# A spectral block kernel: normalized rows in a tile of their own, the second sequence's forward stages due later, one copy on ScalarE

## The chip, the cores and the metric

The kernel runs on one core of a Trainium2 chip. The core has TensorE (PE in the profile; PEld is its weight load), VectorE (DVE), ScalarE (ACT), GpSimd (POOL) and SyncE (SP), which here only issues DMA transfers. The metric is device time in microseconds of one launch.

## The reference

Eight sequences of 3136 rows of 256 float32 values go through two blocks. The second works on the output of the first.

```python
X = np.fft.rfft(x, axis=1)                    # over the rows
Yr = Xr @ w_r - Xi @ w_i + b_r
Yi = Xr @ w_i + Xi @ w_r + b_i
Y  = soft_threshold(Yr, 0.01) + 1j * soft_threshold(Yi, 0.01)
y  = np.fft.irfft(Y, n=3136, axis=1)          # output of the first block
...
mixed = np.real(fft(fft(y, axis=1), axis=2))  # over rows and columns
u  = y + mixed
un = (u - mean(u)) / np.sqrt(var(u) + 1e-6)   # over the columns
out = u + np.maximum(un @ w_ch1, 0) @ w_ch2   # 256 -> 1024 -> 256
```

`soft_threshold` stands for the two lines that shrink a value towards zero by 0.01. The weights `w_ch1` and `w_ch2` come to the kernel as 64-bit floats, which it converts itself.

## The kernel before

A transform over 3136 rows is done as 64 times 49. Every sequence passes through these steps, each a Python generator:

- `p1` (lines 339 to 371), the first forward stage: chunks of the input are loaded by SP (`xf`), multiplied by a 64-point transform matrix (L358 in sequence 1, in plain float32; three products of split values in `mm3`, L150 to L152, elsewhere), copied out of PSUM (`ev`, L366, alternately by ScalarE and VectorE) and stored to DRAM (`ad`, L369). Sequence 1 has twelve chunks, each with two loads and two stores.
- `p2_f2` (390 to 449), the second forward stage F2: in four quarters, loads of `ad` (`af`, L403) and of a table, 49-point transforms (L419), then splitting into a high and a low part. In some places the imaginary half is first copied to a tile `im` by ScalarE (L445), which VectorE then adds (L446).
- `p2_w` (451 to 488): products with `w_r` and `w_i` and the soft threshold. The name in PSUM is `g_w`.
- `p2_mix` (490 to 580): the transform over the columns of the spectrum (L538 for sequence 0, L541 and L543 for the others) and sums of its even and odd parts; at the end of a quarter GpSimd makes two sums (L555, L556), two large copies put them in place (L558 on ScalarE for the even half, L559 on VectorE for the odd half), and SP stores the result (`md`, L565 to L579).
- `p2_yt` and `p2_g2` (584 to 643): transposes and the first inverse transform (L636 for sequence 0), stored as `bd` (L642).
- `p3_norm` (654 to 702): SP loads two blocks of `bd` (`bf`, L669) and of `md` (`mt`, L673 and L675); ScalarE and GpSimd split `bf` (`bh`, `bl`); TensorE does the last inverse transform; VectorE adds the mix (L683) and makes the statistics; the normalized rows are written over `mt` (L700).
- `p3_tr` (704 to 721): TensorE transposes the normalized rows (L718), ScalarE and VectorE split them (`uth`, `utl`).
- `p3_mlp1` and `p3_mlp2` (723 to 759): the two MLP products, with `hh` and `hl` between them (L737 on ScalarE, L738 on VectorE), and the output.

Sequence 0 has its own variants: `p1_first`, and single float32 products instead of split ones in `p2_yt`, `p2_g2` and `p2_mix`. While it passes through, the constants are loaded and `weights` (761 to 773) loads the MLP's weights in eight parts and converts each from 64-bit to a split of two 32-bit parts in `split_double` (158 to 189), mostly on VectorE, with temporary tiles of the tags `mt` and `ut`.

The order of work is a plan written out by hand. Every generator yields the time at which its next piece is due, in units of T = 10000, and a heap takes the earliest (lines 776 to 785). One sequence takes one T: the MLP of sequence b is due from b + 2 to b + 3. The due times are built from constants:

```python
SHAPE0, STEP0 = (1.0, 1.069, 0.988), 0.13
SHAPE, STEP1, STEP = (0.395, 0.569, 0.36), 0.2, 0.25
START1, LEAD = 1.77, 1.48
MLAG, NRM, TR = 0.874, -1.239, -0.993
```

`clock2` (373 to 377) turns them into a start and a step for each quarter of the `p2` stages: sequence 0 starts at 1.0 T with a step of 0.13 T, sequence 1 at `START1` with `STEP1`, later sequences at b + 0.52 T with 0.25 T. SHAPE gives the length of F2, the start of W and the length of W, in steps. `clock3` places normalization, transposes and the MLP of a sequence. `p1` of sequence 1 is due in twelve chunks from 1.4 T over 0.38 T. The framework then assigns instructions to the queues with a simulated timeline, so that instructions can stand a little before or behind their due order; each engine's queue is worked off in order, SP's too. Semaphores between the engines come from the accesses to tiles.

Tiles with one tag share that tag's buffers. Tag `mt` has two buffers of 512 float32 values per partition and is used by the weights' conversion, a constant or two, and `p3_norm`. Tag `im` has two buffers. PSUM tiles `g` have four.

Of the kernel before, what the change touches and what calls it, by code (L numbers as in the profile page):

```python
# [10 lines left out]
F32 = mybir.dt.float32  # L11
# [3 lines left out]
ALU = mybir.AluOpType  # L15
# [4 lines left out]
D = 256  # L20
# [6 lines left out]
S = 50  # L27
# [92 lines left out]
T = 10000  # L120

SHAPE0, STEP0 = (1.0, 1.069, 0.988), 0.13
SHAPE, STEP1, STEP = (0.395, 0.569, 0.36), 0.2, 0.25
START1, LEAD = 1.77, 1.48
MLAG, NRM, TR = 0.874, -1.239, -0.993


# [1 line left out]
def spectral_block(ctx: ExitStack, tc: tile.TileContext, x, w_ri, b_ri, w1, w2,  # L129
# [28 lines left out]
    def split_double(name, h, l, sl, src):  # L158

        def tmp(tag, bufs, dt=I32):
            return sb.tile([128, 512], dt, tag=tag, bufs=bufs, name=f"cv_{name}_{tag}")

        raw = sb.tile([128, 1024], I32, tag="uth", bufs=2, name="raw_" + name)
        behind(1, out=raw.rearrange("p (f e) -> p f e", f=src.shape[1]), in_=src)
        lo, hi = raw[:, 0::2], raw[:, 1::2]
        tf = tmp("mt", 2, F32)
        sc.activation(tf, hi.bitcast(F32), AF.Abs)
        va.tensor_scalar(tf, tf, HI_MIN, HI_MAX, op0=ALU.max, op1=ALU.min)  # L170
        t = tf.bitcast(I32)
        va.tensor_scalar(t, t, 3, 0x7FFFFFFF, op0=ALU.logical_shift_left, op1=ALU.bitwise_and)
        w = tmp("ut", UTB)
        va.tensor_scalar(w, hi, -0x80000000, 0x40000000, op0=ALU.bitwise_and, op1=ALU.bitwise_or)
        va.tensor_tensor(w, w, t, op=ALU.bitwise_xor)
        wf = w.bitcast(F32)
        e = tmp("ut", UTB)
        va.tensor_scalar(e, w, -0x800000, None, op0=ALU.bitwise_and)
        r = tmp("mt", 2)
        va.tensor_scalar(r, lo, 8, None, op0=ALU.logical_shift_right)  # L180
        rf = tmp("ut", UTB, F32)
        va.scalar_tensor_tensor(rf, r, 2.0 ** -44, e.bitcast(F32), op0=ALU.mult, op1=ALU.mult)

        def v(t):
            return t.rearrange("p (f e) -> p f e", f=h[sl].shape[1]) if len(h[sl].shape) == 3 else t
        sc.copy(h[sl], v(wf))
        d = tmp("ut", UTB, F32)
        gp.tensor_sub(v(d), v(wf), h[sl].bitcast(F32))
        gp.tensor_add(l[sl], v(d), v(rf))
# [15 lines left out]
    def load_consts():  # L205
        yield 0.97 * T
        behind("x", out=fwd_f, in_=c_fwd)
        w_v = w_ri.rearrange("a (k p) e -> a p k e", p=128)
        for name, tag in (("wr", "hh"), ("ws", "hh"), ("wd", "hl")):
            KF[name] = sb.tile([128, 2, D], F32, tag=tag, bufs=2, name=name + "f")  # L210
        behind("x", out=KF["wr"], in_=w_v[0])
        wi = sb.tile([128, 2, D], F32, tag="mt", bufs=2, name="wi")
        behind("x", out=wi, in_=w_v[1])

        for name, sign in (("ws", -1.0), ("wd", 1.0)):
            va.scalar_tensor_tensor(KF[name], wi, sign, KF["wr"], op0=ALU.mult, op1=ALU.subtract)
        for name in ("wr", "ws", "wd"):
            split(name, KF[name])
        yield 0.99 * T
        KF["cs"] = sb.tile([128, 2, 129], F32, tag="hl", bufs=2, name="csf")  # L220
        behind("x", out=KF["cs"], in_=c_cs)
        yield 1.55 * T
        split("fwd", fwd_f)

        cs = K["cs"] = cp.tile([128, 2, 2, 128], F32R, name="cs")
        t = KF["cs"]
        sc.copy(cs[:, :, 0], t[:, :, 0:128])
        lo_v(cs[:, :, 1], t[:, :, 0:128], cs[:, :, 0])
        sc.copy(cs[:, 0, 1, 0:1], t[:, 0, 128:129])
        inv = sb.tile([128, 128], F32, tag="mt", bufs=2, name="inv_f")  # L230
        nc.sync.dma_start(out=inv, in_=c_inv)
        split("inv", inv)

# [105 lines left out]
    def p1(b):  # L339
# [6 lines left out]
                ad = dr.tile([N2, 2, U, D], F32, tag="ad", bufs=4, name=f"ad{i}")  # L346
                a_dram[i] = lambda u, ad=ad: (ad, u)
        todo = chunks + [(NM - 1, 1)] * (b % 2 == 0)
        t0, width = (1.4, 0.38) if b == 1 else (b - 0.3, 0.75)
        for ci, (m, n) in enumerate(todo):  # L350
            yield T * (t0 + width * ci / len(todo))
            w = n * D
# [37 lines left out]
    def p2_f2(b):  # L390


        for q in range(4):
# [17 lines left out]
            for ui in range(4):  # L411
# [23 lines left out]
                if ui < (3 if b else 2):  # L435
                    xx = sb.tile([128, 2, 2, 2, S], F32, tag="xx", bufs=2, name="xx")
                    xv_ = xx.rearrange("p k s c j -> p k s (c j)")
                    sc.copy(xv_, gv)
                    put(sc.copy, [Xh], xv_)
                    put(lo_g, [Xl, Xh], xv_)  # L440
                    va.tensor_add(xs, xx[:, :, :, 0], xx[:, :, :, 1])
                else:
                    im = sb.tile([128, 2, 2, S], F32, tag="im", bufs=2, name="im")
                    put(sc.copy, [Xh], gv)
                    sc.copy(im, gv[:, :, :, S:])  # L445
                    va.tensor_add(xs, gv[:, :, :, :S], im)  # L446
                    put(lo_v, [Xl, Xh], gv)
# [42 lines left out]
    def p2_mix(b):  # L490
# [12 lines left out]
        for q in range(4):  # L503
# [52 lines left out]
            gp.tensor_sub(mq[:, 0, :, 1, 1:], even[:, :, 1:], odd[:, :, 1:])  # L556
            sc.copy(mq[:, 0, :, 0, 0:1], even[:, :, 0:1])
            sc.copy(even[:, :, 1:], mq[:, 0, :, 1, 1:])  # L558
            va.tensor_copy(odd[:, :, 1:], mq[:, 0, :, 0, 1:])  # L559
            sc.copy(odd[:, :, 0:1], mq[:, 0, :, 1, 0:1])  # L560
            mr = mq.rearrange("p a u h e -> p a (u h e)")
            mp, mm = (mq[:, i].rearrange("p u h e -> p u (h e)") for i in range(2))
# [91 lines left out]
    def p3_norm(b):  # L654

        for gi, (g0, z) in enumerate(groups[b % 2]):
            t0, T3 = clock3(b, g0)
            for i, n in parts_of[z]:
# [5 lines left out]

                src = [(b - 1, m), (b, m)] if joint else [(b, m), (b, NM + m)]
                bf = sb.tile([128, 512], F32, tag="bf", bufs=2, name="bf")
                mt = sb.tile([128, 2, D], F32, tag="mt", bufs=2, name="mt")
                for r, (bb, n2) in enumerate(src):
                    nc.sync.dma_start(out=bf[r * 64:r * 64 + 64, :w].rearrange("p (n d) -> p n d", d=D),  # L669
                                      in_=n2_rows(b_dram[bb], n2, n))  # L670
# [25 lines left out]
                gp.tensor_mul(vv[:, :n], vv[:, :n], rs[:, :n])  # L696
                gp.tensor_scalar(vv[:, :n], vv[:, :n], -0.5, 1.5, op0=ALU.mult, op1=ALU.add)
                gp.tensor_mul(rs[:, :n], rs[:, :n], vv[:, :n])  # L698
                for j in range(n):
                    va.tensor_scalar(mt[:, j], ut[:, j], ag[:, j, 0:1], rs[:, j], op0=ALU.subtract, op1=ALU.mult)  # L700
                normed[b, gi, i] = mt
                uts[b, gi, i] = ut

    def p3_tr(b):
        for gi, (g0, z) in enumerate(groups[b % 2]):
            t0, T3 = clock3(b, g0)
            for i, n in parts_of[z]:
                yield t0 + T3 * (TR + i / 4)
                if i == 0:
                    uth = sb.tile([128, 2, 512], F32R, tag="uth", bufs=2, name="uth")  # L710
                    utl = sb.tile([128, 2, 512], F32R, tag="utl", bufs=2, name="utl")
                    uthl[b, gi] = uth, utl
                mt = normed.pop((b, gi, i))
                g = gtile("g_ut")
                gv = g.rearrange("p (k t) -> p k t", k=2)
                for j in range(n):
                    for k in range(2):
                        te.transpose(gv[:, k, j * 128:(j + 1) * 128], mt[:, j, k * 128:(k + 1) * 128], ident)  # L718
                tw = slice(i * 128, i * 128 + n * 128)
                sc.copy(uth[:, :, tw], gv[:, :, :n * 128])  # L720
                lo_v(utl[:, :, tw], gv[:, :, :n * 128], uth[:, :, tw])
# [101 lines left out]
```

## Time and profile before

| | us |
|---|---|
| median of 3 runs | 1958.12 |
| lowest and highest run | 1956.15, 1961.05 |
| the profiled execution, its time | 1961.45 |
| the profiled execution, its span | 1959.7 |

| engine | busy us | share of the span |
|---|---|---|
| TensorE, matmuls | 1856.2 | 95% |
| TensorE, weight loads | 1709.1 | 87% |
| VectorE | 1322.5 | 67% |
| ScalarE | 853.2 | 44% |
| GpSimd | 704.8 | 36% |

The granted TensorE clock is 0.969 on the mean of the span. The profile shows one execution. A line of the timeline gives start and duration in us, the engine, the kernel's line, the operation, its output and inputs by the program's names, and in brackets how long the engine was idle before it and what ended that. SPq is SyncE's queue of DMA issues; the duration there is that of the issue, not of the transfer. Ends of matmuls are modelled, so a busy TensorE is not one at its peak.

### The profile page before, as it was taken

The numbers are of one execution on the slowest core, as the hardware profiler recorded it, in microseconds if no ns is written. First come the engines' busy times: TensorE is split into PE (matmuls) and PEld (weight loads), VectorE is DVE, ScalarE is ACT, GpSimd is POOL, SyncE is SP. The second block draws the span as 40 slices with busy tenths as digits, with TensorE's granted clock in tenths as the row PEclk, the third lists the DMA queues.
The fourth block names the chain that finished last, engine by engine and source line by source line (L and its number), as shares of the span: only waits on it lengthen the run. The fifth ranks groups of instructions, "written<-read, shape, count | busy, mean of one in ns | idle before, by whom it ended". The sixth has DMA issues, their size and how long they took to land.

```text
span 1959.7 us, 35047 instructions
## 1 busy us (share of the span) xinstructions
PE 1856.2 (95%) x12115; PEld 1709.1 (87%) x12115; DVE 1322.5 (67%) x2831; ACT 853.2 (44%) x1888; POOL 704.8 (36%) x1087
## 2 busy tenths in 40 slices
PE   4875799999999999999999999999999999999999
PEld 3764699989999999998999999998999998998999
DVE  2676677777776777766677777766777766675543
ACT  2443544444444454443444544434544434433322
POOL 0345544344433444343333443323543322322210
PEclk7886899999999999999999999999999999999999
DMA  7466654345443544434443444435433332223210
GB/s 215 122 177 192 154 139 131 101 119 148 115 122 109 152 129 121 117 98 138 136 134 104 136 137 114 127 99 141 136 106 98 107 98 89 83 70 109 68 41 25
DMA packets 163540, 233.05 MB, mean 119 GB/s; under 512 B 27484, under 2 KB 107428, under 8 KB 163364
## 3 DMA queue, kind: packets, MB, share of 16 engines
q1 hardware_dynamic: 163364, 230.82, 41.9%
q8 instruction: 97, 1.59, 0.3%
q14 instruction: 79, 0.65, 0.1%
HBM read 127.95 MB, written 102.76 MB: 118 GB/s over the span
## 4 chain that ended last, share of the span: by engine, by line
PE 80%; DVE 7%; DMA 6%; SPq 3%; issue 2%; ACT 1%; POOL 1%; DVEq 0%; POOLq 0%; ACTq 0%
PE o L150 8%; PE o L151 8%; PE o L152 8%; PE h L150 8%; PE h L151 8%; PE h L152 8%; PE g_f L419 4%; PE g_w L150 3%; PE g_w L152 3%; PE g_w L151 3%; PE g_g L150 2%; PE g_g L152 2%; PE g_g L151 2%; PE g_yt L609 2%; PE g_ut L718 2%
## 5 line engine op out<-in xcount | busy, mean ns | idle before, releaser
L151 PE MATMUL o<-w2h,hl 128*128 128x256 f32 x1568 | 431.4, 285 | 8.4 <-DVE hl L738 8.4
L738 DVE SCALAR_TENSOR_TENSOR hl<-h,hh 128x512 fp32r<-128x512 f32 (+1 forms) x416 | 272.3, 655 | 243.8 <-ACT hh L737 242.5
L737 ACT ACTIVATE hh<-h 128x512 fp32r<-128x512 f32 (+1 forms) x416 | 238.0, 573 | 443.0 <-PE h L152 382.7
L152 PE MATMUL o<-w2h,hh 128*128 128x256 f32 x1568 | 424.2, 280 | 0.0
L150 PE MATMUL o<-w2l,hh 128*128 128x256 f32 x1568 | 397.6, 286 | 2.5 <-DVE ut L757 2.3
L150 PE MATMUL h<-utl,w1h 128*128 128x512 f32 (+1 forms) x832 | 323.5, 389 | 8.1 <-DVE hl L738 8.1
L152 PE MATMUL h<-uth,w1h 128*128 128x512 f32 (+1 forms) x832 | 317.0, 381 | 0.0
L151 PE MATMUL h<-uth,w1l 128*128 128x512 f32 (+1 forms) x832 | 316.6, 381 | 0.0
L151 PEld LDWEIGHTS o<-w2h,hl 128*128 128x128 f32 x1568 | 297.3, 190 | 14.8 <-DVE hl L738 10.3
L152 PEld LDWEIGHTS o<-w2h,hh 128*128 128x128 f32 x1568 | 297.0, 189 | 3.2
L150 PEld LDWEIGHTS o<-w2l,hh 128*128 128x128 f32 x1568 | 286.3, 189 | 15.1 <-ACT Xsh L428 2.9
L147 POOL TENSOR_TENSOR bl<-bf,bh 128x512 fp32r<-128x512 f32 x104 | 130.0, 1251 | 298.3 <-ACT bh L678 296.1
L419 PE MATMUL g_f<-tff,af 98*128 98x100 f32 x1024 | 155.2, 284 | 25.8 <-DMA tff<-c_tf 13.0
L419 PEld LDWEIGHTS g_f<-tff,af 98*128 98x128 f32 x1024 | 148.5, 204 | 34.2 <-issue 23.4
L152 PEld LDWEIGHTS h<-uth,w1h 128*128 128x128 f32 x832 | 156.8, 189 | 23.8
L150 PEld LDWEIGHTS h<-utl,w1h 128*128 128x128 f32 x832 | 157.0, 189 | 22.8 <-DVE hl L738 9.0
L147 POOL TENSOR_TENSOR xl<-xf,xh 128x512 fp32r<-128x512 f32 (+1 forms) x75 | 97.1, 1295 | 203.2 <-ACT xh L362 201.3
L151 PEld LDWEIGHTS h<-uth,w1l 128*128 128x128 f32 x832 | 157.3, 189 | 13.4
L683 DVE TENSOR_TENSOR ut<-g_g,mt 128x512 f32<-128x512 f32 x104 | 68.3, 657 | 104.9 <-PE g_g L152 67.9
L147 POOL TENSOR_TENSOR Xl<-xx,Xh 128x400 fp32r<-128x400 f32 (+1 forms) x96 | 106.3, 1110 | 89.6 <-ACT Xh L428 69.3
L147 POOL TENSOR_TENSOR Xsl<-xs,Xsh 128x200 fp32r<-128x200 f32 x120 | 76.9, 642 | 161.4 <-ACT Xsh L428 144.2
L700 DVE TENSOR_SCALAR mt<-ut,ag,rs 128x256 f32<-128x256 f32 x196 | 90.8, 502 | 48.9 <-POOL rs L698 48.6
(155 smaller groups left out, 3811.3 us busy)
## 6 DMA issues: line engine op xcount, KB each, us to landing
bd<-bev SPq DMA_DIRECT2D x128, 196.0 KB
af<-ad SPq DMA_DIRECT2D x62, 392.0 KB
bf<-bd SPq DMA_DIRECT2D x184, 128.0 KB
out_dram<-ut SPq DMA_DIRECT2D x92, 256.0 KB
xf<-in_x SPq DMA_DIRECT2D x176, 128.0 KB
ad<-ev SPq DMA_DIRECT2D x168, 128.0 KB
md<-mq SPq DMA_DIRECT2D x112, 192.0 KB
mt<-md SPq DMA_DIRECT2D x416, 32.0 KB
```

What stands on the lines that cost most here:

```text
L147: gp.tensor_sub(out_, full, hi.bitcast(F32))
L150: te.matmul(o, lh, rl, start=start, stop=False)
L151: te.matmul(o, ll, rh, start=False, stop=False)
L152: return te.matmul(o, lh, rh, start=False, stop=stop)
L419: te.matmul(g[:, o:o + 100], afs[s][:, ui * D + k * 128:ui * D + k * 128 + 128], tfs[s][:, ui], start=True, stop=True)
L609: te.transpose(gt[:100, (v * 2 + o) * 128:(v * 2 + o + 1) * 128], y[:, o, place].rearrange("p c j -> p (c j)"), ident)
L683: va.tensor_add(ut[:, :n], g[:, :w].rearrange("p (n d) -> p n d", d=D), mt[:, :n])
L700: va.tensor_scalar(mt[:, j], ut[:, j], ag[:, j, 0:1], rs[:, j], op0=ALU.subtract, op1=ALU.mult)
L718: te.transpose(gv[:, k, j * 128:(j + 1) * 128], mt[:, j, k * 128:(k + 1) * 128], ident)
L737: sc.activation(hh[:, :w], h[:, :w], AF.Relu)
L738: va.scalar_tensor_tensor(hl[:, :w], h[:, :w], 0.0, hh[:, :w].bitcast(F32), op0=ALU.max, op1=ALU.subtract)
```

## The change

Four things are changed.

1. `p3_norm` writes the normalized rows to a new tile `nm` instead of over `mt`, and `p3_tr` transposes `nm`. The new tile shares the tag `mt`, which gets three buffers instead of two everywhere. So `mt` itself is written by DMAs alone, and is read once.
2. The due times of sequence 1's two forward stages: `p1` from 1.56 T over 0.34 T (it was 1.4 T over 0.38 T); `START1` is 1.92 (1.77) and `STEP1` 0.175 (0.2), which holds for all of sequence 1's `p2` stages.
3. The tag `im` has one buffer instead of two.
4. For sequence 0 the copy of the odd half of the mix (L559) is on ScalarE; for the others it stays on VectorE.

```diff
-SHAPE, STEP1, STEP = (0.395, 0.569, 0.36), 0.2, 0.25
-START1, LEAD = 1.77, 1.48
+SHAPE, STEP1, STEP = (0.395, 0.569, 0.36), 0.175, 0.25
+START1, LEAD = 1.92, 1.48
...
-        tf = tmp("mt", 2, F32)
+        tf = tmp("mt", 3, F32)
...
-        t0, width = (1.4, 0.38) if b == 1 else (b - 0.3, 0.75)
+        t0, width = (1.56, 0.34) if b == 1 else (b - 0.3, 0.75)
...
-                    im = sb.tile([128, 2, 2, S], F32, tag="im", bufs=2, name="im")
+                    im = sb.tile([128, 2, 2, S], F32, tag="im", bufs=1, name="im")
...
-            va.tensor_copy(odd[:, :, 1:], mq[:, 0, :, 0, 1:])
+            (va.tensor_copy if b else sc.copy)(odd[:, :, 1:], mq[:, 0, :, 0, 1:])
...
-                mt = sb.tile([128, 2, D], F32, tag="mt", bufs=2, name="mt")
+                mt = sb.tile([128, 2, D], F32, tag="mt", bufs=3, name="mt")
...
+                nm = sb.tile([128, 2, D], F32, tag="mt", bufs=3, name="nm")
                 for j in range(n):
-                    va.tensor_scalar(mt[:, j], ut[:, j], ag[:, j, 0:1], rs[:, j], op0=ALU.subtract, op1=ALU.mult)
-                normed[b, gi, i] = mt
+                    va.tensor_scalar(nm[:, j], ut[:, j], ag[:, j, 0:1], rs[:, j], op0=ALU.subtract, op1=ALU.mult)
+                normed[b, gi, i] = nm
...
-                        te.transpose(gv[:, k, j * 128:(j + 1) * 128], mt[:, j, k * 128:(k + 1) * 128], ident)
+                        te.transpose(gv[:, k, j * 128:(j + 1) * 128], nm[:, j, k * 128:(k + 1) * 128], ident)
```

The other lines with the tag `mt` change its number of buffers only.

More of the change, by code (lines that the diff above doesn't have):

```diff
@@ L178, in split_double @@
         va.tensor_scalar(e, w, -0x800000, None, op0=ALU.bitwise_and)
-        r = tmp("mt", 2)
+        r = tmp("mt", 3)
         va.tensor_scalar(r, lo, 8, None, op0=ALU.logical_shift_right)
@@ L211, in load_consts @@
         behind("x", out=KF["wr"], in_=w_v[0])
-        wi = sb.tile([128, 2, D], F32, tag="mt", bufs=2, name="wi")
+        wi = sb.tile([128, 2, D], F32, tag="mt", bufs=3, name="wi")
         behind("x", out=wi, in_=w_v[1])
@@ L229, in load_consts @@
         sc.copy(cs[:, 0, 1, 0:1], t[:, 0, 128:129])
-        inv = sb.tile([128, 128], F32, tag="mt", bufs=2, name="inv_f")
+        inv = sb.tile([128, 128], F32, tag="mt", bufs=3, name="inv_f")
         nc.sync.dma_start(out=inv, in_=c_inv)
@@ L712, in p3_tr @@
                     uthl[b, gi] = uth, utl
-                mt = normed.pop((b, gi, i))
+                nm = normed.pop((b, gi, i))
                 g = gtile("g_ut")
```

## The prediction

> **What bounds the kernel now.** I read the page's strip of slices first, then the stages by windows, then TensorE's order of work in the one stage with gaps, and last the queues that hold it there.
>
> ```profile
> span 1959.7 us, 35047 instructions
> ...
> PE   4875799999999999999999999999999999999999
> ...
> PEclk7886899999999999999999999999999999999999
> ```
>
> ```profile
> 86.00:135.00 49.00, 40.31 (x185) 32.22 (x184) 39.93 (x77) 25.81 (x66) 24.44 (x24) 0.86 0.64 184
> 135.00:182.00 47.00, 27.90 (x91) 19.12 (x92) 29.89 (x51) 17.24 (x36) 18.50 (x13) 0.68 0.70 212
> 182.00:224.00 42.00, 21.26 (x96) 18.66 (x96) 21.40 (x39) 15.18 (x33) 21.03 (x29) 0.67 0.61 156
> 224.00:440.00 216.00, 212.92 (x1432) 196.40 (x1432) 168.40 (x343) 106.41 (x237) 93.70 (x132) 1.00 0.45 124
> ```
>
> The columns after the stretch are busy time of PE, PEld, DVE, ACT and POOL, then the granted clock. From 224 us on TensorE is busy 212.92 of 216 us at full clock, and the strip stays at 9 to the end. What is done there costs its full TensorE time and can hardly gain. Before 224 us TensorE idles 9, 19 and 21 us of the three stretches, at a clock of 0.86 to 0.67. So the end moves by one balance: how much earlier the saturated part begins, less the TensorE work that is no longer done by then. The saturated part begins with the first MLP product of sequence 0.
>
> ```profile
> 167.74 1.42 PE L358 MATMUL g_f<-xf,fwd_f 128*128 128x512 f32 x2
> ...
> 173.45 0.39 PE L152 MATMUL g_f<-xh,fwdh 128*128 128x512 f32 x1
> 177.48 1.15 PE L419 MATMUL g_f<-tff,af 98*128 98x100 f32 x4 [3.63 <-DMA af<-ad]
> 178.42 1.91 PE L636 MATMUL g_g<-yf,tif 100*98 100x256 f32 x4
> 180.12 1.07 PE L538 MATMUL g_mix<-csf,ef 128*100 128x129 f32 x4
> ...
> 208.63 0.66 PE L718 MATMUL g_ut<-ident,mt 128*128 128x128 f32 x2 [12.01 <-DVE mt L700]
> ...
> 213.46 0.44 PE L150 MATMUL g_w<-Xl,wsh 128*128 128x400 f32 x1
> ...
> 215.64 0.35 PE L152 MATMUL g_w<-Xh,wdh 128*128 128x400 f32 x1
> 217.36 0.41 PE L718 MATMUL g_ut<-ident,mt 128*128 128x128 f32 x2 [1.37 <-issue]
> ...
> 220.52 0.38 PE L718 MATMUL g_ut<-ident,mt 128*128 128x128 f32 x2
> ...
> 223.85 0.47 PE L150 MATMUL h<-utl,w1h 128*128 128x512 f32 x1
> ```
>
> TensorE works in order. At 177.48 us it stands for the first matmul of sequence 1's F2, and behind it stand the last inverse product (L636) and the last mix (L538) of sequence 0, on which normalization waits. Then 12 us pass at the first transpose, and 15.2 us more until the MLP starts at 223.85.
>
> ```profile
> 185.99 5.81 DVE L559 COPY mq<-mq 100x508 f32<-100x508 f32 x1 [1.16 <-POOL mq L556]
> ...
> 202.51 0.69 DVE L683 TENSOR_TENSOR ut<-g_g,mt 128x512 f32<-128x512 f32 x1 [10.71 <-DMA mt<-md]
> ```
>
> ```profile
> 188.15 0.61 ACT L558 COPY mq<-mq 100x508 f32<-100x508 f32 x1
> ```
>
> ```profile
> 189.02 2.50 POOL L147 TENSOR_TENSOR bl<-bf,bh 128x512 fp32r<-128x512 f32 x2
> ```
>
> ```profile
> 185.90 0.47 SPq L262 DMA_DIRECT2D tif<-c_ti  x1
> 191.87 0.32 SPq L565 DMA_DIRECT2D md<-mq  x1
> ...
> 198.32 0.33 SPq L673 DMA_DIRECT2D mt<-md  x1
> ```
>
> This is the chain in those 12 us: the copy at L559, the mix's store at 191.87, the load of it at 198.32, the addition at 202.51.
>
> **The copy on ScalarE.**
>
> ```profile
> L559 DVE COPY mq<-mq x32: 408/417/5811, 98.7 to 1765.3; 100x508 f32<-100x508 f32 x32
> ```
>
> The columns are lowest, median and highest duration in ns. The median is 0.42 us, the one on the chain 5.81. It ends at 191.80, right behind GpSimd's last of a run of operations (189.02 + 2.50 = 191.52). On ScalarE the like copy of the other half (L558) took 0.61 us in the same place, so the odd copy should too. ScalarE was late itself: L558 ended at 188.76. Behind it the odd copy ends at 189.4, which gains 2.4 us; begun at 185.99, as VectorE's was, it would gain 191.80 - 185.99 - 0.61 = 5.2. I take 3.0, nearer to the lower, since ScalarE's order holds casts that wait for loads. It adds a wait for GpSimd there, with the short copy of L560 and casts queued behind. The other three copies cost 0.2 us more each and stand beside other work.
>
> The Trainium skill (SBUF — State Buffer, "Who interferes with whom") says that VectorE and GpSimd share a port pair under an exclusive lock held for a whole instruction, and that ScalarE never waits. By that rule as worded the copy would lose one GpSimd instruction (2.50 / 2 = 1.25 us) and then run (0.42); moving it would gain about 1.1 us, and the sum below would be -5.0 instead of -6.9. The trace disagrees, since the copy was locked out to the end of the run, so this gets no chance of its own.
>
> **The first forward stage of sequence 1 (12 chunks of p1) moves** from 1.40..1.748 T to 1.56..1.872 T (T is the plan's unit, one sequence). Each chunk issues two loads and two stores on SP.
>
> ```profile
> L262 SPq DMA_DIRECT2D xf<-in_x x30: 466/521/1517, 89.3 to 177.6; - x30
> ```
>
> ```profile
> L369 SPq DMA_DIRECT2D ad<-ev x28: 574/622/1098, 91.3 to 175.9; - x28
> ```
>
> That is 2 x 0.52 + 2 x 0.62 = 2.3 us of SP a chunk, and 24 records of 0.75 us for 12 chunks, 1.5 us of TensorE each, with 11.2 us of idle time before them in all:
>
> ```profile
> L358 PE MATMUL g_f<-xf,fwd_f 128*128 128x512 f32 x24 | 15.9, 749 | 11.2 <-DMA ad<-ev 4.8 <-issue 3.2 <-ACT w2h L186 2.1
> ```
>
> Before 1.56 T six chunks leave (6 x 2.3 = 13.7 us of SP). Between there and the last mix of sequence 0 (1.784 T) there are eight instead of six, and four come behind it. What the six leave behind them matters through the weights:
>
> ```profile
> 141.66 1.67 SPq L262 DMA_DIRECT2D raw_w<-in_w  x2
> ```
>
> ```profile
> 145.71 1.25 DVE L174 TENSOR_SCALAR cv_w_ut<-raw_w 128x512 int32<-128x512 int32 x1 [0.16 <-DMA raw_w<-in_w]
> ...
> 168.12 0.69 DVE L182 SCALAR_TENSOR_TENSOR cv_w_ut<-cv_w_mt,cv_w_ut 128x512 f32<-128x512 int32 x1
> ```
>
> The second weight's raw data, due from 1.45 T, is loaded only at 141.66 us, behind chunks on SP, and its conversion fills VectorE from 145.71 to 168.8; ScalarE's casts wait for it, and TensorE's work behind them. With six chunks fewer in front, these loads come earlier into a stretch where VectorE idles 9 us of 49. The gain lies between 0 (the first stretch is not held by SP) and 13.7 (all of it is). Two more chunks later take 2 x 2.3 = 4.6 of that back at most. I take -5.0 net, near a third of the 13.7.
>
> **The second forward stage (F2, W and what follows)** starts at 1.92 T instead of 1.77, with a step of 0.175 T for 0.2. Sequence 0's last products are due at 1.777 and 1.784 T, so F2 now stands behind them. TensorE then reaches L636 at 173.45 + 0.39 = 173.84 instead of 178.42: -4.6 (0 if ScalarE's or a load's wait takes its place). W of the first quarter was due from 1.849 T and is due from 1.989. So it leaves the 15.2 us between first transpose and MLP: the second pair of transposes came at 220.52, 3.2 us behind the first pair at 217.36, with W's products between, and VectorE's W operations stood in the same queue. I take -3.5 (0 to -5).
>
> What the earlier start gives up: 36 products of W and a few of F2 move into the saturated part. Twelve run from 213.46 to 215.64 at 0.19 us apart, so 36 x 0.19 = 6.8 us, with eight F2 matmuls (about 0.9 us) +7.7. The chunks of p1 and the first quarter of F2 (due 1.92 to 1.98 T) still come before 2.0 T and move nothing.
>
> **The handover to normalization of sequence 1.**
>
> ```profile
> 426.81 0.69 DVE L683 TENSOR_TENSOR ut<-g_g,mt 128x512 f32<-128x512 f32 x1 [1.51 <-DMA mt<-md]
> ```
>
> The last mix of sequence 1 was due at 1.77 + 0.6 + 0.2 x 1.927 = 2.755 T and is at 1.92 + 0.525 + 0.175 x 1.927 = 2.782 T; normalization stays at 2.802. From 223.85 us (2.0 T) to 426.81 (2.802 T) a T is 253 us, so 6.8 us of slack go. VectorE already waited 1.5 us there. While it waits at L683, the hl subtractions (L738) queue behind it, and TensorE waits for hl. Cost 0 to +6.8; I take +1.0, since the MLP's product is due 0.2 T later.
>
> **The tiles.** A normalized row block now takes the third buffer of the tag. If buffers go round, the load two blocks on still waits for the same transposes, and a block's own load comes no earlier.
>
> ```profile
> PE g_ut L718 <- DVE mt L700: 13.2, 4, 12.0
> ```
>
> TensorE lost 13.2 us at the transposes, 12.0 of it at the first, where no buffer was short; so 0 to -1.2, taken as 0. With one `im` buffer, ScalarE's second `im` copy of a quarter of sequence 0 waits for VectorE's L446, with a cast (L428) queued behind:
>
> ```profile
> L446 DVE TENSOR_TENSOR xs<-g_f,im 128x200 f32<-128x200 f32 x9 | 3.3, 362 | 2.9 <-POOL Xsl L147 1.4 <-PE g_w L150 0.8 <-POOL Xl L147 0.7
> ```
>
> Four such waits of at most 0.36 us are 0 to +1.4; I take +0.5. Later sequences use `im` once a quarter, where the earlier use is long past.
>
> **The sum.** -3.0 - 5.0 - 4.6 - 3.5 = -16.1 for the earlier start; +7.7 + 1.0 + 0.5 = +9.2 against it; together -6.9. The profiled execution took 1961.45 us (span 1959.7), which gives 1954.6. It is 3.3 us above the median of the runs, 1958.12, so for the median I say 1951.2. What a measurement can tell from no change is 0.3%, 5.9 us.
>
> **Rivals.** *Slower: SP becomes the bound of the new place.* The six chunks' 13.7 us of SP time stand later, eight chunks in the tail of sequence 0's mix and four between its stores and normalization's loads, and SP works in order: a chunk's store waits for its copy, and the mt loads behind it. For it: in 182 to 224 us VectorE's 10.71 us wait at L683 ends with such a load. Against it: SP stood still for the 5.5 us between 186.37 and 191.87, and issues of four chunks replace those of F2. Its price: the -5.0 goes (the sum is then -1.9) and up to 13.7 comes, +11.8, or 1970. It decides from 7.8 us of the 13.7 on. Chance 0.19.
>
> *No change: the transfers set the start anyway.* The way from store to addition (191.87 to 202.51) stays, and what comes ahead is absorbed in it: -5.0 and -3.5 go, leaving -7.6 + 9.2 = +1.6, or 1959.7. For it: the chain there is DMA and waits, not work. Against it: the store's own time is set by the copy and the mix ahead of it. Chance 0.25.
>
> *Larger gain: the weights' conversion leaves the chain.* -13.7 instead of -5.0 gives -15.6, or 1942.5. For it: TensorE idles 19 of 47 us in just that stretch. Chance 0.12.
>
> **How the numbers follow.** The forecast, 1951.2, has 0.44; its own range is 1946 to 1956 from the bounds of the copy and of W's place. About 0.38 of it lies beyond 5.9 us, which with the larger gain makes 0.50 faster. Slower is the SP rival, 0.19; the rest, 0.31, lies within. The range goes from 1941, just past the larger gain, to 1964, which takes in no change and the nearer half of the slower case.
>
> **What would show it.** Right: the last L538 ahead of sequence 1's first L419; the odd copy on ScalarE at about 0.6 us and the first store of the last mix at once behind; the second weight's conversion begun before 140 us; the first MLP product some 12 to 19 us before 223.85, with W's first products behind it; from there to 440 us TensorE as full as now. Wrong: the first MLP product at 220 or later, SP's loads of mt behind stores of chunks, or a gap of several us on TensorE at the handover near 420.

## The result and the profile after

| | median us | lowest, highest | runs |
|---|---|---|---|
| before | 1957.13 | 1954.13, 1961.05 | 4 |
| after | 1984.43 | 1976.19, 1991.09 | 4 |

After to before the ratio is 1.0136, 95% interval 1.0092 to 1.018. The kernel became 27 us slower (18 to 35 by the interval), where 7 us faster was forecast (1951.2) and 1964 was the end of the range. The profiled execution of the changed kernel took 1986.48 us, with a span of 1984.7 and the same mean clock as before, 0.969. In the changed kernel the lines behind 698 have a number higher by one.

The windows of the changed kernel, in the same stretches (columns as in the prediction):

```profile
86.00:135.00 49.00, 32.33 (x161) 26.66 (x160) 38.51 (x69) 23.74 (x63) 25.56 (x24) 0.83 0.43 133
135.00:182.00 47.00, 29.11 (x105) 19.18 (x103) 31.27 (x55) 19.99 (x44) 19.06 (x13) 0.75 0.70 197
182.00:224.00 42.00, 15.15 (x35) 8.86 (x36) 9.07 (x21) 9.55 (x17) 12.17 (x19) 0.58 0.65 178
224.00:440.00 216.00, 211.21 (x1399) 195.97 (x1398) 161.08 (x335) 104.74 (x236) 89.98 (x128) 0.99 0.43 119
```

The third row is the loss at the start: 35 TensorE records instead of 96, and VectorE busy for 9.07 us instead of 21.40. Some 40 of these records are products of sequence 1's F2 and W that the change means to move behind the start of the MLP; the rest is time lost. The chunks that left the first stretch show there as a DMA share of 0.43 instead of 0.64, and as nothing else that got faster. TensorE's order of work in the place of the loss:

```profile
178.96 0.61 PE L538 MATMUL g_mix<-csf,ef 128*100 128x129 f32 x4
...
199.45 0.69 PE L719 MATMUL g_ut<-ident,nm 128*128 128x128 f32 x2 [4.14 <-DVE nm L701]
...
208.96 0.79 PE L150 MATMUL g_f<-xl,fwdh 128*128 128x512 f32 x1 [5.45 <-POOL xl L147]
...
210.40 0.63 PE L150 MATMUL g_g<-bl,invh 128*128 128x512 f32 x1
...
220.84 0.66 PE L719 MATMUL g_ut<-ident,nm 128*128 128x128 f32 x2 [8.96 <-DVE nm L701]
...
229.60 0.39 PE L150 MATMUL h<-utl,w1h 128*128 128x512 f32 x1
```

The first transpose comes 9.2 us earlier than before (199.45 for 208.63), and the MLP starts 5.75 us later (229.60 for 223.85). So 15.2 us between the two have become 30.15. Only this distance can be relied on: single traces put the whole start a few us earlier or later. Two traces of one and the same kernel below (mt3_only, mt3_1280) start the MLP at 222.12 and 229.03 us, and pad_only, which changes no due time, has its first transpose at 198.12. The distance is 12.6 to 16.3 us in all twelve traces with the due times of before, and 30.1 in a second trace with the changed ones (after_1280). The second block's product starts at 210.40, no earlier than before (210.37), although the first block is earlier, and its transposes at 220.84 come later than the 217.36 of before. ScalarE's queue shows by what:

```profile
184.08 0.61 ACT L559 COPY mq<-mq 100x508 f32<-100x508 f32 x1
...
206.95 0.62 ACT L362 CAST xh<-xf 128x512 fp32r<-128x512 f32 x1 [3.14 <-DMA xf<-in_x]
...
215.20 0.62 ACT L362 CAST xh<-xf 128x512 fp32r<-128x512 f32 x1 [7.64 <-DMA xf<-in_x]
215.73 0.29 ACT L691 ACTIVATE rs<-ag,eps_t 128x2 f32<-128x2 f32 x1
```

The casts of L362 belong to chunks of sequence 2 (those of sequence 1 are not cast). Each waits for a load, and the first keeps TensorE from the second block's product until 208.96 + 1.44 = 210.40, the second keeps its `rs` until 215.73. In the issues of that stretch, 182 to 224 us, before and after, chunk loads have become 15 instead of 4:

```profile
xf<-in_x SPq DMA_DIRECT2D x4, 128.0 KB
```

```profile
xf<-in_x SPq DMA_DIRECT2D x15, 128.0 KB
```

The second half of the loss shows in no gap. The 128x256 products of the second MLP matmul, before and after (columns: busy us, mean ns, idle before):

```profile
L152 PE MATMUL o<-w2h,hh 128*128 128x256 f32 x1568 | 424.2, 280 | 0.0
```

```profile
L152 PE MATMUL o<-w2h,hh 128*128 128x256 f32 x1568 | 429.6, 283 | 0.0
```

There are three such forms, 4704 matmuls. From the starts of some 4000 pairs of neighbours that follow without a gap, the next one comes 115.8 ns after the last before the change and 118.4 ns after the change; 4704 times 2.6 ns is 12.2 us. Which matmuls these are, and why they are slower, the experiments had to show.

### The profile page after: what moved, and what is told of

Same layout as the page of the kernel before. It is cut to its first block, busy times and chain, and to the rows that moved or that the text cites. A ratio compares the mean times of both kernels' runs of the same rounds, so it can differ in the third digit from the quotient of the medians.

```text
span 1984.7 us, 34704 instructions
## 1 busy us (share of the span) xinstructions
PE 1866.7 (94%) x12115; PEld 1715.7 (86%) x12115; DVE 1308.9 (66%) x2827; ACT 854.4 (43%) x1892; POOL 702.9 (35%) x1087
## 4 chain that ended last, share of the span: by engine, by line
PE 79%; DVE 5%; DMA 4%; SPq 2%; ACT 1%; issue 1%; POOL 1%; DVEq 0%; POOLq 0%; ACTq 0%
PE o L151 9%; PE o L150 8%; PE o L152 8%; PE h L150 8%; PE h L152 8%; PE h L151 8%; PE g_f L419 4%; PE g_w L150 3%; PE g_w L152 3%; PE g_w L151 3%; PE g_g L150 2%; PE g_yt L609 2%; PE g_g L152 2%; PE g_g L151 2%; PE g_ut L719 2%; PE g_mix L541 1%
## 5 line engine op out<-in xcount | busy, mean ns | idle before, releaser
L151 PE MATMUL o<-w2h,hl 128*128 128x256 f32 x1568 | 436.8, 287 | 7.3 <-DVE hl L739 6.9
L152 PE MATMUL o<-w2h,hh 128*128 128x256 f32 x1568 | 429.6, 283 | 0.0
L701 DVE TENSOR_SCALAR nm<-ut,ag,rs 128x256 f32<-128x256 f32 x196 | 88.7, 491 | 60.8 <-POOL rs L698 60.3
```

The lines of the kernel that those rows point to most:

```text
L151: te.matmul(o, ll, rh, start=False, stop=False)
L152: return te.matmul(o, lh, rh, start=False, stop=stop)
L701: va.tensor_scalar(nm[:, j], ut[:, j], ag[:, j, 0:1], rs[:, j], op0=ALU.subtract, op1=ALU.mult)
```

## The experiments

Each version was timed beside the kernel before on the same chip. Single executions of one kernel lie 10 us and more apart (before: 1949.6 to 1963.5 over all series), so the medians decide, and a trace is used for where things stand.

| version | median us | before us | ratio, 95% interval |
|---|---|---|---|
| copy_only | 1955.92 | 1958.43 | 0.9991, 0.9974 to 1.0008 |
| tile_only | 1980.20 | 1958.43 | 1.0108, 1.0088 to 1.0127 |
| late_only | 1977.48 | 1958.43 | 1.0094, 1.0077 to 1.0111 |
| tile_copy | 1976.99 | 1958.43 | 1.0092, 1.0075 to 1.0108 |
| pad_only | 1968.56 | 1956.97 | 1.0053, 1.0032 to 1.0074 |
| mt3_only | 1976.22 | 1956.97 | 1.0096, 1.0078 to 1.0115 |
| late_f2 | 1964.26 | 1956.97 | 1.0030, 1.0015 to 1.0045 |
| late_p1 | 1978.37 | 1956.97 | 1.0106, 1.0083 to 1.0130 |
| pad_32 | 1967.65 | 1956.72 | 1.0060, 1.0042 to 1.0077 |
| tile_1280 | 1970.70 | 1956.72 | 1.0074, 1.0052 to 1.0096 |
| im_only | 1956.65 | 1956.72 | 1.0001, 0.9989 to 1.0013 |
| copy_all | 1947.79 | 1956.72 | 0.9955, 0.9938 to 0.9971 |
| after_1280 | 1975.47 | 1957.55 | 1.0092, 1.0071 to 1.0113 |
| mt3_1280 (= mt3_only) | 1976.88 | 1957.55 | 1.0094, 1.0073 to 1.0114 |
| late_p1_p2 | 1967.14 | 1957.55 | 1.0053, 1.0037 to 1.0070 |
| copy_all_p2 | 1940.68 | 1957.55 | 0.9914, 0.9896 to 0.9933 |
| mt3_pad32 | 1965.39 | 1957.80 | 1.0041, 1.0023 to 1.0060 |
| best_pad64 | 1954.03 | 1958.19 | 0.9986, 0.9973 to 0.9999 |

Differences in us below are a ratio's excess times 1957.

### Which part costs it

Three theories: the later due times cost it (D), the new tile costs it (T), or any edit shifts the queues and costs something (R).

**The copy alone.**

```diff
-            va.tensor_copy(odd[:, :, 1:], mq[:, 0, :, 0, 1:])
+            (va.tensor_copy if b else sc.copy)(odd[:, :, 1:], mq[:, 0, :, 0, 1:])
```

> The kernel before with one change: the odd copy of sequence 0 on ScalarE. Theory D (the later due times cost the time): faster by 3 to 7 us against before, since in the changed kernel the store of the last mix left at 184.75 us and not at 191.87. Theory T (the new tile costs it): the same 3 to 7 us faster. Theory R (any edit reorders the queues, and the order found is a matter of luck): anything from 8 us faster to 15 us slower.

Measured -1.8 us (-5.1 to +1.6): no loss, and a gain that can't be told from none.

**The tile alone**: `nm`, three buffers of `mt`, one of `im`.

> The kernel before with the tile nm, three buffers of tag mt and one of im; due times and copy as before. Theory D: within 6 us of before. Theory T: slower by 12 us or more, with the loads of mt later at the first blocks. Theory R: anything within 15 us.

**The due times alone**: `p1` of sequence 1, `START1` and `STEP1`.

> The kernel before with the later due times of sequence 1's two forward stages alone (p1 at 1.56 T, START1 1.92, STEP1 0.175). Theory D: slower by 25 to 35 us against before, the first MLP product at 230 to 240 us and 90 to 110 matmuls fewer done by 250 us. Theory T: slower by less than 12 us. Theory R: slower by 0 to 20 us.

**All but the due times.**

> The changed kernel with the due times of before (tile and copy stay). Theory D: faster than before by 2 to 8 us, so 30 us faster than the changed kernel. Theory T: slower than before by 5 us or more. Theory R: not the sum of the copy alone and the tile alone.

The tile costs +21 (17 to 25), the due times +18 (15 to 22), all but the due times +18 (15 to 21). So neither D nor T is the cause alone: two halves, each about as large. D also missed the size of its own half (+18, not 25 to 35, with the first MLP product at 224.02). R fell: tile and copy together cost what they cost alone (+18 for 21 - 2), and the tile alone lies beyond R's 15 us. Together they would be more than the changed kernel's +27, whose interval ends at 35; that the two losses overlap is likely, but was not shown.

### The tile's half: the place in memory

The tile changes no due time, and TensorE was slower by a steady 2.5 ns a matmul, so the first suspect was where the tiles lie. Three buffers of `mt` (+2048 bytes per partition) and one of `im` (-800) move the tiles of most tags that are first used later by 1248 bytes, the second weight's `w2h` and `w2l` among them; `hh` and `hl` stay.

**A tile that nobody uses, and nothing else.**

```diff
+        pad = sb.tile([128, 312], F32, tag="pad", bufs=1, name="pad")
+        gp.memset(pad, 0.0)
         wi = sb.tile([128, 2, D], F32, tag="mt", bufs=2, name="wi")
```

> The kernel before with one unused tile of 1248 bytes per partition ahead of the tag mt. From mt on, all tiles of later tags stand 1248 bytes higher, as they do with the three buffers of mt and the one of im; nothing else is changed. In the runs with the tile the 128x256 matmuls of the second MLP product start 2.4 ns later behind one another than before in quiet stretches, 4704 x 2.4 ns = 11 us of the +21. Theory P (the place of the tiles in memory slows these matmuls): +8 to +12 us here, and their mean goes from 280 to 283 ns. Theory Q (the order in the queues, which the new tile changes, makes all of it): 0, within 3 us of before, mean 280 ns. Theory B (the number of buffers itself): 0 as well.

Measured +10 us (6 to 14). Theory P held: 118.3 ns from start to start, as with the tile. Of the matmuls outside `o`, the pairs most frequent in the trace (`h`, `g_f`, `g_yt`, `g_ut`) kept their distance within 0.2 ns; of these, `h` and `g_yt` have operands that don't move, so only the other two say anything.

**Three buffers of `mt` and one of `im`, without `nm`.**

> The tag mt with three buffers and im with one, but the normalized rows still written over mt. TensorE's queue is that of before but for some 20 places, and the tiles stand at the addresses of the changed kernel. Theory P (place in memory): +8 to +12 us, the 128x256 matmuls at 283 ns. Theory B (a third buffer lets loads run ahead and collide, or the single im costs): +15 us or more, as with the new tile. Theory Q (only the new tile, since only it changes the order in the queues): within 3 us of before.

Measured +19 (15 to 23): nearly the tile's whole loss, with the rows still written over `mt`. So more than the place is lost without `nm`.

**A pad of 32 bytes.** The diff is that of the first pad, with 8 values instead of 312.

> The kernel before with one unused tile of 32 bytes per partition ahead of the tag mt. The second weight's tiles w2h and w2l begin at 193,440 and 201,632 bytes in the kernel before, 32 bytes past a multiple of 64; with the pad of 1248 bytes they began at a multiple of 64, every row of them alike cost the 128x256 matmuls 2.5 ns more, and the median rose by 10 us. Theory A (the address within 64 bytes decides): here they begin at a multiple of 64 too: +8 to +12 us, and o<-w2h,hh at 282 ns. Theory D (the distance decides, by which region of the memory the tiles come to lie in): a shift of 32 bytes does nothing, within 3 us of before and 280 ns.

+12 (8 to 15), theory A. A shift of 32 bytes does what the shift of 1248 did; it is not which region of the memory the tiles lie in. The rows of `w2h` are 1024 bytes apart, so each has the same address within 128 bytes.

**The tile with a pad of 32 bytes**, which moves the rest by 1280 bytes instead of 1248.

```diff
+        pad = sb.tile([128, 8], F32, tag="pad", bufs=1, name="pad")
+        gp.memset(pad, 0.0)
         wi = sb.tile([128, 2, D], F32, tag="mt", bufs=3, name="wi")
```

> The new tile with three buffers of mt and one of im, due times and copy as before, and an unused tile of 32 bytes ahead of mt: the tiles behind it are moved by 1280 bytes instead of 1248, so w2h and w2l lie 32 bytes past a multiple of 64 as in the kernel before. Theory A (address within 64 bytes): the 128x256 matmuls are back at 280 ns, and of the tile's +21 us about 11 go: +8 to +12. Theory D (distance): +18 to +22 as with the tile alone.

+14 (10 to 19), 7 less than the tile alone; theory A expected up to +12. The matmuls are back at 280 ns:

```profile
L152 PE MATMUL o<-w2h,hh 128*128 128x256 f32 x1568 | 424.3, 280 | 0.0
```

**The same in the changed kernel.**

> The changed kernel with an unused tile of 32 bytes ahead of mt, so that w2h and w2l lie 32 bytes past a multiple of 64 again. Theory A (the address within 64 bytes costs 4704 matmuls 2.5 ns each): 10 to 13 us less than the changed kernel, that is +13 to +18 over before, and o<-w2h,hh at 280 ns instead of 283. If the place matters only together with the other due times: +22 to +28.

+18 (14 to 22) where the changed kernel had +27 (18 to 35). The intervals overlap, but the row shows the effect itself: 280 ns, where the changed kernel had 283.

```profile
L152 PE MATMUL o<-w2h,hh 128*128 128x256 f32 x1568 | 425.2, 280 | 0.0
```

**A pad of 64 bytes** on the fastest version (below).

> The fastest version so far (the copy of the odd half on ScalarE for all sequences, sequence 2's chunks from 2.0 T over 0.45 T; -16.9 us) with an unused tile of 64 bytes ahead of mt: w2h and w2l begin 96 bytes past a multiple of 128, which is again 32 past a multiple of 64. Theory A64 (64 bytes decide): o<-w2h,hh at 279 to 280 ns and 1938 to 1944 us. Theory A128 (only 32 past a multiple of 128 is fast): 282 ns and 1949 to 1955 us.

Theory A64 fell, A128 held: +13 us against the 1940.68 of another series, and

```profile
L152 PE MATMUL o<-w2h,hh 128*128 128x256 f32 x1568 | 430.0, 283 | 0.0
```

with 119.0 ns from start to start. Together, by where `w2h` begins past a multiple of 128 bytes: at 0 (pad_only, the tile, the changed kernel) 118.3 to 118.4 ns; at 32 (before, tile_1280, after_1280, mt3_pad32) 115.7 to 115.9; at 64 (pad_32) 118.2; at 96 (best_pad64) 119.0. `hh` and `hl`, the other operand, began at 96 in all runs. Whether the address itself decides or its distance from the other operand's was not tried.

### The tile's half: the rest

**One buffer of `im` alone**, with a pad of 800 bytes so that nothing behind `im` moves.

```diff
-                    im = sb.tile([128, 2, 2, S], F32, tag="im", bufs=2, name="im")
+                    im = sb.tile([128, 2, 2, S], F32, tag="im", bufs=1, name="im")
```

> The kernel before with one buffer of im, and an unused tile of 800 bytes so that all tiles behind it stay where they are. With three buffers of mt and one of im the time rose by 19 us, of which the place in memory explains 10. Theory I (the single im makes the other 9: ScalarE's second copy of a quarter waits for VectorE's addition, with the casts for W behind it): +6 to +10 us. Theory M (the third buffer makes it: loads run ahead and change what stands in the queues): within 3 us of before.

+0.2 us (-2 to +3): the single `im` costs nothing.

**Three buffers of `mt` without the change of place.** The run under the label mt3_1280 was given the kernel without the small pad, so it only repeats mt3_only (+18, 14 to 22); the kernel meant is mt3_pad32.

> Three buffers of mt, one of im, rows still written over mt, and the unused tile of 32 bytes. Without that tile it was +19, of which 11 are the place. Theory M (a third buffer alone costs the other 8, by another order of loads): +6 to +10. Theory Q (the rest needs the new tile): within 3 us of before. The single im alone has been measured at nothing.

> Three buffers of mt, one of im, rows still written over mt, and the unused tile of 32 bytes, so that w2h and w2l lie 32 bytes past a multiple of 64 as before. Without the small tile this kernel was +19 in two series. Theory M (the third buffer by itself costs what the place doesn't explain): +6 to +10. Theory Q (the rest needs the new tile): within 3 us of before.

+8 (4 to 12): theory M. The third buffer costs something by itself. What the new tile adds to that, tile_1280 less mt3_pad32, is about 6, and the intervals overlap. What the tile changes is seen in SP's waits (us in total, times, longest). Before, with mt3_pad32, and with tile_1280 (whose line numbers are higher by two):

```profile
SPq L673 <- PE g_ut L718: 137.6, 54, 6.0
SPq L669 <- POOL bl L147: 81.9, 27, 9.6
```

```profile
SPq L675 <- PE g_ut L720: 106.0, 41, 6.0
SPq L671 <- POOL bl L147: 75.8, 23, 9.6
```

```profile
SPq L671 <- POOL bl L147: 138.0, 35, 9.6
...
SPq L675 <- PE g_ut L721: 3.9, 3, 3.2
```

SP hardly waits for transposes any more before it loads `mt`. The dependency is still there: in the built program the tag's three buffers go round, and a load of `mt` waits for the transposes of the rows two blocks back. But in SP's queue a load of `mt` now mostly stands behind the `bf` loads of three further blocks, where it stood behind those of two. SP waits there for a `bf` buffer, and by then the transposes are mostly done. TensorE gains nothing by that, and at the handover near 430 us the queues' new order is seen to hurt. ScalarE and TensorE with tile_only:

```profile
430.67 0.62 ACT L678 CAST bh<-bf 128x512 fp32r<-128x512 f32 x1 [4.20 <-DMA bf<-bd]
...
431.62 0.59 ACT L738 ACTIVATE hh<-h 128x512 fp32r<-128x512 f32 x1
```

```profile
432.26 0.50 PE L150 MATMUL o<-w2l,hh 128*128 128x256 f32 x2 [3.27 <-ACT hh L738]
```

A normalization cast stands for a load of `bf` ahead of `hh`, and TensorE waits 3.27 us (4.17 in tile_copy, 3.60 in tile_1280). Before, the gap there was 0.77 us, and 1.85 to 1.87 in copy_only, im_only, pad_only and pad_32. So it is 1 to 3 us at that one place; how the 14 us are made up was not settled.

### The due times' half

**The second stage alone** (`START1`, `STEP1`).

> The kernel before with START1 1.92 and STEP1 0.175 alone; the first forward stage of sequence 1 stays at 1.4 T. Theory S (the moved chunks cost it: their loads are slow, and their casts stand in ScalarE's queue ahead of the second block's normalization): the first MLP product comes before 218 us and the time is -3 to +4 us. Theory G (the work given up costs it: F2 and W of sequence 1 leave the gaps, and the MLP does not start earlier for it): first MLP product at 222 to 226 us, +8 to +15 us. Theory H (the later second stage meets the normalization of sequence 1): a gap of 4 us or more on TensorE between 400 and 450 us.

+6 us (3 to 9), between theory S (up to +4) and theory G (from +8). TensorE's order in late_f2:

```profile
194.62 0.66 PE L718 MATMUL g_ut<-ident,mt 128*128 128x128 f32 x2 [8.32 <-DVE mt L700]
...
203.24 0.66 PE L718 MATMUL g_ut<-ident,mt 128*128 128x128 f32 x2 [5.18 <-issue]
203.69 1.87 PE L419 MATMUL g_f<-tff,af 98*128 98x100 f32 x8
...
211.76 1.86 PE L419 MATMUL g_f<-tff,af 98*128 98x100 f32 x8
...
214.74 0.42 PE L150 MATMUL h<-utl,w1h 128*128 128x512 f32 x1
```

W's products have left the place between the first transpose and the MLP, but the 32 matmul records of sequence 1's first F2 quarter stand there in their stead, as they do in the changed kernel (221.30 to 229.04). The distance is 20.1 us, where it was 15.2, and 41 matmul records fewer are done when the MLP begins (581 for 622; 36 of W and 8 of F2 fewer, 3 others more). The MLP itself starts at 214.74; that is 9.1 us earlier than in the trace of before, but inside the 213.56 to 229.03 of the nine traces with the copy and the due times of before, so it isn't shown that the start is earlier at all. Windows of before, of im_only (whose time and due times are those of before) and of late_f2:

```profile
0.00:250.00 250.00, 171.35 (x801) 139.95 (x802) 144.59 (x280) 104.33 (x248) 93.23 (x118) 0.79 0.61 172
...
350.00:450.00 100.00, 97.64 (x650) 89.46 (x650) 74.09 (x151) 46.18 (x103) 41.55 (x58) 1.00 0.44 124
```

```profile
0.00:250.00 250.00, 169.77 (x822) 138.64 (x823) 145.43 (x285) 104.74 (x250) 91.76 (x119) 0.80 0.62 173
...
350.00:450.00 100.00, 95.71 (x639) 87.68 (x639) 72.91 (x146) 45.62 (x102) 41.30 (x58) 1.00 0.42 118
```

```profile
0.00:250.00 250.00, 172.26 (x806) 139.00 (x807) 139.66 (x280) 104.44 (x244) 95.29 (x122) 0.81 0.61 169
...
350.00:450.00 100.00, 95.08 (x617) 87.35 (x616) 67.44 (x139) 41.25 (x94) 35.56 (x50) 0.97 0.34 96
```

Against before alone, the start would break even (806 records for 801) and the loss would come in 350 to 450 us, at the handover to sequence 1. Against im_only it is the other way round: 16 records fewer by 250 us, and only 0.6 us less of TensorE's busy time at the handover. So single traces don't tell where the 6 us arise. Theory H fell (the longest gap from 350 to 450 us was 2.65 us), and G's reason, that the earlier start is paid for with work given up, is neither shown nor refuted.

**The first stage alone** (`p1` from 1.56 T over 0.34 T).

> The kernel before with the twelve chunks of sequence 1 due from 1.56 T over 0.34 T alone; START1 and STEP1 as before. Theory S (the chunks in the new place cost it): first MLP product at 226 us or later, +10 to +20 us, with ScalarE at a cast of xf for several us between the two normalizations of the first blocks. Theory G (only the second stage's delay costs): within 4 us of before.

+21 (16 to 25), theory S, just past its range. TensorE and ScalarE of late_p1:

```profile
199.64 0.69 PE L718 MATMUL g_ut<-ident,mt 128*128 128x128 f32 x2 [0.45 <-DVE mt L700]
...
212.17 7.12 PE L419 MATMUL g_f<-tff,af 98*128 98x100 f32 x32 [8.77 <-DMA af<-ad]
...
220.41 0.63 PE L150 MATMUL g_g<-bl,invh 128*128 128x512 f32 x1
...
235.73 0.48 PE L150 MATMUL h<-utl,w1h 128*128 128x512 f32 x1
```

```profile
206.84 0.62 ACT L362 CAST xh<-xf 128x512 fp32r<-128x512 f32 x1 [3.69 <-DMA xf<-in_x]
215.94 0.62 ACT L678 CAST bh<-bf 128x512 fp32r<-128x512 f32 x1 [8.48 <-DMA bf<-bd]
```

Late chunks are stored late (SP issues the last stores of `ad` ahead of F2 from 204.66), `af` is loaded from `ad` behind them at 207.76, F2 of sequence 1 waits 8.77 us for that load, and F2 stands in TensorE's queue ahead of the second block's `g_g`. The MLP starts 36.1 us behind the first transpose, where it was 15.2. With F2 later as well (late_only, the changed kernel) F2 no longer stands there, and the two due times together cost +18, not 21 + 6.

**Are the chunks of sequence 2 to blame, that got pushed there?**

```diff
-        t0, width = (1.4, 0.38) if b == 1 else (b - 0.3, 0.75)
+        t0, width = (1.56, 0.34) if b == 1 else (2.0, 0.45) if b == 2 else (b - 0.3, 0.75)
```

> The chunks of sequence 1 due from 1.56 T over 0.34 T, and those of sequence 2 from 2.0 T over 0.45 T instead of 1.7 T over 0.75 T, so that none of sequence 2 is due before the MLP of sequence 0. With sequence 1's chunks alone the first MLP product came at 235.73 us and the time rose by 21 us; between the two normalizations ScalarE stood at casts of sequence 2's chunks and of bf, each waiting for its load. Theory C (sequence 2's chunks, pushed there, hold up normalization): first MLP product before 222 us, time -2 to +8. Theory L (sequence 1's late chunks hold it up by themselves, by their transfers and SP's queue): first MLP product at 228 us or later, +12 to +20.

+10 (7 to 14), with the MLP at 224.28: between the two theories. Half of the loss goes, but a run below (copy_all_p2 against copy_all) shows that the same remedy is worth 8 us where nothing was late, so only the rest of some 2 us, less than the intervals can tell from none, belongs to chunks of sequence 2 that were pushed. The distance from first transpose to MLP stays as it was in late_p1, 36.3 us. F2 still waits ahead of `g_g`:

```profile
200.49 7.12 PE L419 MATMUL g_f<-tff,af 98*128 98x100 f32 x32 [7.99 <-DMA af<-ad]
207.31 0.77 PE L150 MATMUL g_g<-bl,invh 128*128 128x512 f32 x1
```

So theory L, sequence 1's late chunks by themselves, holds the larger part.

### A faster version

**The copy for all sequences.**

```diff
-            va.tensor_copy(odd[:, :, 1:], mq[:, 0, :, 0, 1:])
+            sc.copy(odd[:, :, 1:], mq[:, 0, :, 0, 1:])
```

> The kernel before with the copy of the odd half (L559) on ScalarE for all eight sequences. For sequence 0 alone the time was 2.5 us lower, which the interval doesn't tell from nothing. Theory K (the copies that VectorE can't begin or finish beside GpSimd hold up the handovers too): -3 to -8 us. Theory N (at the handovers ScalarE's queue, with casts that wait for loads, is no better a place): -3 to +3 us.

-9 us (-12 to -6), just past theory K's range. SP's waits for the copy, before and in copy_all:

```profile
SPq L565 <- DVE mq L559: 52.5, 17, 14.9
```

```profile
SPq L565 <- ACT mq L559: 10.3, 8, 6.7
```

**With sequence 2's chunks behind the start**, `(2.0, 0.45) if b == 2` as above, and `p1` of sequence 1 as before:

> The copy of the odd half on ScalarE for all sequences, -8.9 us by itself, and sequence 2's chunks due from 2.0 T over 0.45 T. Theory C: they leave the start too: -12 to -16 against before. Theory L: what leaves the start is done in the saturated part instead, 12 chunks of 0.7 us at most, and SP meets the stores there: -4 to -9.

-17 us (-20 to -13), just past theory C's range. 1940.68 is the fastest of all versions here, and the MLP starts 11.6 us behind the first transpose, where it is 15.6 in copy_all:

```profile
211.84 0.39 PE L150 MATMUL h<-utl,w1h 128*128 128x512 f32 x1
```

Whether sequence 1's chunks would do better still earlier is open: a version with its `p1` from 1.3 T gave no kernel, since the plan orders each chunk's load behind an `af` load of sequence 0's last quarter, due only at 1.39 T.

## Why the prediction was wrong

**The step that failed first: "The first forward stage of sequence 1 moves", taken as -5.0.** Alone it is +21. Two premises broke. Six chunks less in the first stretch were to bring the second weight's load forward by up to 13.7 us of SP's time; it came at 139.91 us instead of 141.66, and its conversion began at 144.29 instead of 145.71:

```profile
139.91 1.08 SPq L262 DMA_DIRECT2D raw_w<-in_w  x2
```

```profile
144.29 0.43 DVE L174 TENSOR_SCALAR cv_w_ut<-raw_w 128x512 int32<-128x512 int32 x1 [1.74 <-DMA raw_w<-in_w]
```

SP's issues did not hold that load. With the chunks gone SP stands still instead; its longest wait from 84 to 150 us, ahead of a table load at 115.34, is

```profile
SPq L262 <- PE g_g L636: 7.2, 1, 7.2
```

And the new place was costed only by SP's issue time, 4.6 us. What counted there was the wait of in-order queues for the transfers: ScalarE's at casts of chunks and of `bf`, TensorE's at F2. The slower rival was right in its direction and its place, and wrong in its engine and its price: it priced SP's issues at +11.8 in all.

**The second failed step: "The tiles", taken as 0.** Its argument went by buffers, and they do go round as it assumed; but SP's queue was reordered, and the waits for transposes went from 137.6 us to 3.9 (tile_1280), into waits for `bf`. The cost, +21, lay where no step looked: 7 to 12 in the address of a tile that the diff doesn't name (7 given back by tile_1280, 10 and 12 lost by the pads), about 8 with the third buffer, the rest with the new tile itself.

**The copy**, -3.0: 0.61 us on ScalarE as predicted, and the store of the last mix came 7.1 us earlier in the changed kernel than before (191.87):

```profile
184.75 0.31 SPq L565 DMA_DIRECT2D md<-mq  x1
```

That this is the copy's work isn't shown: with the copy on VectorE the same store leaves at 181.33 in pad_only and at 186.64 in pad_32. The 5.81 us on which the term was built were a long case, too: VectorE's longest copy is 4.0 to 4.3 us in im_only, pad_only, pad_32, mt3_only, mt3_pad32, tile_only and tile_1280. Alone the copy brought -1.8, within its uncertainty the predicted size, and also within it nothing. "The other three copies" and, by the median of 0.42 us, all later ones were taken as standing beside other work; copy_all says that the 28 others are worth about 7 us. The median of the copy's duration hides what matters: 52.5 us of SP's waits for it, in the wait table that the prediction did not read for this copy.

**F2 and W**: -4.6 - 3.5 + 7.7 for the start and +1.0 for the handover are +0.6; late_f2 measured +6 (3 to 9). The -3.5 failed in its mechanism: it counted W's products leaving the distance between first transpose and MLP, and not F2's coming in, whose first quarter it took to "move nothing", and the distance grew from 15.2 to 20.1 us. The +7.7 had its count right: 36 products of W and 8 of F2 are done later. How the rest of the +6 is shared among the terms is open. Some due times in this step were off, without effect on it: by the code W of the first quarter was due from 1.884 T and is due from 2.020, not 1.849 and 1.989, and the slack lost at the handover is 7.0 us, not 6.8.

**The single `im`**, +0.5: measured +0.2, as taken.

**The result of the sum.** An earlier first transpose was part of the forecast (the first MLP product 12 to 19 us earlier), and the 9.2 us of the traces go that way, but pad_only's 198.12 shows that they may be chance. The forecast failed behind it, in the 15.2 us to the MLP, from which it took 3.5 away and which became 30.15.

## What to carry to other kernels

What is moved to a later due time brings its loads along, and in a queue worked off in order everything behind it waits for them: cost a moved stage by the waits for its transfers in the new place, and follow who reads what it stores. When a tile or a buffer is added, compare the addresses of the operands of the hottest matmuls before and after; a shift of 32 bytes cost this kernel 12 us, and an unused tile of 32 bytes gave the changed kernels 7 to 9 back. Look at who waits for an instruction, not at its median duration, before calling it covered. And before a time in one trace is called earlier or later, look for it in a second trace of the same order of work; here the distance between two events held within some 4 us where the events themselves moved by 15.

## What the runs showed of the hardware that was not expected

The 128x256 matmuls of fp32r operands follow one another after 115.8 ns if the moving operand's rows begin 32 bytes past a multiple of 128, and after 118.2 to 119.0 ns at 0, 64 or 96 bytes past it, with the other operand at 96 throughout. The Trainium skill (SBUF — State Buffer, "Operand start alignment") asks only that an operand start at a multiple of its element size, and says of its rule that it is "about legality, not speed". The runs here add a speed: 2 to 3% of these matmuls, 10 to 13 us of this kernel. What in the memory makes the difference, no run here shows.
